# Softplus taken from its table on h itself, 64-bit weights converted with a Prelu, a shift and a join, and a new order of the work

## The chip, the cores and the metric

The kernel runs on one core of one Trainium2 chip. The metric is device time in microseconds (us) of one execution; lower is better. A core has a matrix engine (TensorE, called PE in the profile; PEld is its weight load, which overlaps PE), a vector engine (VectorE, DVE), a scalar engine for activations (ScalarE, ACT), a general engine (GpSimd, POOL) and a queue that issues DMAs (SyncE, SP). Each engine works through its own instructions in the order in which the program lists them; semaphores hold an instruction until what it needs is there.

## The reference

Attention with a forget gate, then two MLPs over its output. Batch 4, 8 heads, 576 positions, head size 64; 2304 tokens of width 512; hidden width 2048. The MLP weights come as 64-bit floating point numbers.

```python
scores = scale * q @ k.T + (cum[:, None] - cum[None, :])   # cum = cumsum(log(clip(f, 1e-4, 1)))
attn = softmax(where(causal, -1e9, scores))
x = attn @ v                                               # to [2304, 512]
h = x @ w_in;  g = maximum(h, 0) + alpha * minimum(h, 0);  x = g @ w_out
h = x @ w_in2; g = maximum(h, 0) + log1p(exp(-abs(h)));    out = g @ w_out2
```

The last `g` is softplus(h).

## The kernel before

The 32 heads are worked in 16 pairs (`pair`, 9 query tiles each). A tile gets its scores from PE, the decay from POOL, the row maximum from DVE (line 643), the exponential `p` from ACT (line 651); PE turns `p` (line 660), and the turned tile is split into a rounded part and a rest (lines 681 and 685), which PE multiplies with `v` (line 725).

The MLPs work on chunks of 384 tokens (6 chunks, three of them from the first half of the batch) and on groups of 4 blocks of 128 hidden units. One slot is one block of one chunk. `hidden` computes `h` in PSUM by 12 matmuls (line 889, the same count in both MLPs), applies the nonlinearity, and splits the result into `g`: ACT casts the rounded part (line 925), DVE subtracts it for the rest (line 928). `product` multiplies `g` with `wout` (line 946): 128x384 per matmul in the first MLP, 9 matmuls of 128x512 a slot in the second. `total` adds the groups (lines 965, 967). The second MLP has 96 slots; in its stage there are 3 PSUM banks for `h` and 6 buffers for `g`. The first three chunks of the first MLP run beside the second half of attention.

In the second MLP the nonlinearity is softplus: DVE sets the sign bit of `h` (line 911, result `ta`, that is -|h|), ACT applies the Softplus table to `ta` (line 915), DVE adds max(h, 0) (line 918).

`weights` turns 64-bit weights into a rounded 32-bit part and a rest. One conversion handles 128x512 numbers: a DMA to `raw` (lines 386, 391); ACT scales the upper words by 2^-112 (`lower`, line 394, result `ca`); DVE shifts (line 397, result `cu`) and joins the sign (line 401); ACT rounds `cu` into the first part (line 413); DVE takes the bits below out of the words (line 405), joins them with the lower word (line 409), takes the power of two (line 416) and multiplies (line 420). There are 64 conversions: 32 for each MLP. Those of the first MLP are also stored to DRAM and read again for the second half of the chunks.

The order is set by a planner (`Plan`). Each step has an engine, a length, the things that it reads and writes, and a rank made from the numbers of `TUNE`. `emit` runs a clock: each free engine takes the step of lowest rank whose inputs are there and for whose results there is a buffer. What comes out is a fixed list for each engine. The planner has no step for a load of activation tables; such a load is put in when the program is built, ahead of an activation whose function is not in the table that is loaded.

```python
        plan.add("act", t_act(512), lower, reads=[rkey], writes=[ua], rank=rank)
        plan.add("dve", t_dve(512, True), shift, reads=[ua], writes=[uu], rank=rank, port=True)
```

Of the kernel before, what the change touches and what calls it, by code (L numbers as in the profile page):

```python
# [7 lines left out]
F32 = mybir.dt.float32  # L8
F32R = mybir.dt.float32r
BF16 = mybir.dt.bfloat16  # L10
U32 = mybir.dt.uint32
# [7 lines left out]


TUNE = {
    "TILE1": 0.42, "TILE2": 0.47, "SLOT2": 7.65, "SLOT3": 13.68, "qr": (-5.98, -0.1), "kr": (0.68, -0.52),
    "vr": (-1.32, 560.85), "cum": (11.69, 8.14), "q": (-1.09, -699.23), "k": (-3.93, -2.73),
    "v": (8.47, 0.66), "decay": (-1.18, 0.77), "scores": (0.88, 3.13), "max": (-8.47, 0.3),
    "pad": (-25.9, 9.39), "exp": (79.74, 1.39), "turn": (-0.12, -0.34), "hi": (1.38, 0.0),
    "lo": (2.49, -2.45), "values0": (16.5, 0.87), "values1": (148.3, 515.38), "sum": (3.42, -0.84),
    "finish": (-1.52, 37.07), "sums": (-1.34, -5.25), "blocks": 6.2, "product": 14.59, "total": 1.13,
    "weights": -0.99, "raw": -0.0, "mlp": -1.66,
}


# [164 lines left out]
def t_act(cols, extra=0, sbuf=True):  # L196
    return (0.094 if sbuf else 0.053) + cols / 1200.0 + 0.093 * extra
# [6 lines left out]
def t_dve(cols, fast=False):  # L204
    return 0.07 + cols / (1920.0 if fast else 960.0)
# [11 lines left out]
def forgetting_attention_two_mlps(  # L217
# [43 lines left out]
            "d": [0, 1, 2, 3], "p": [0, 1, 2, 3], "mx": [0, 1, 2, 3], "sm": [0, 1], "xt0": [0], "xt1": [0], "x32": [0, 1], "r": [0],  # L261
            "rd": [0, 1], "rb": [0], "pt": list(range(8)), "ahead": [0, 1, 2, 3],
            **{"P%d%d%d" % (t, x, n): [0] for t in range(len(UNITS)) for x in range(2) for n in range(2)},
            "raw": [0, 1], "ca": [0, 1], "cu": [0, 1], "win": list(range(5)),
            "wout": [], "h": [], "o": [], "g": [], "ta": [],
        },
        ("p", "d", ("pt", "s"), "win", "wout", "raw"),
# [49 lines left out]
    def buf(key):  # L317
        return tiles[key[0], plan.place[key]]
# [43 lines left out]
    def weights(kind, m, ff, key, rank):  # L362
# [5 lines left out]
        if m == 0 and (kind, ff) in kept:  # L368
# [4 lines left out]

            plan.add("sp", 1.3, again, reads=[saved], writes=[key], rank=rank + DUE["raw"], late=2.92)
            return
        rkey, ua, uu = ("raw", key), ("ca", key), ("cu", key)

        def parts():
            words = buf(rkey).bitcast(U32).rearrange("p (n two) -> p n two", two=2)
            halves = buf(rkey).bitcast(U16).rearrange("p (n four) -> p n four", four=4)  # L380
            return words[:, :, 0], words[:, :, 1].bitcast(F32), halves[:, :, 2]

        def load():
            r = buf(rkey)
# [6 lines left out]
                nc.sync.dma_start(out=r, in_=W[m][1][ff * 128:ff * 128 + 128, :])  # L391

        def lower():
            nc.scalar.mul(out=buf(ua), in_=parts()[1], mul=2.0 ** -112)  # L394

        def shift():
            nc.vector.tensor_scalar(out=buf(uu), in0=buf(ua).bitcast(U32), scalar1=3, scalar2=0x7FFFF000,
                                    op0=ALU.logical_shift_left, op1=ALU.bitwise_and)

        def join():  # L400
            nc.vector.scalar_tensor_tensor(out=buf(uu), in0=parts()[1].bitcast(U32), scalar=0x80000000, in1=buf(uu),
                                           op0=ALU.bitwise_and, op1=ALU.bitwise_or)

        def fraction():
            nc.vector.tensor_scalar(out=buf(ua).bitcast(U32), in0=parts()[1].bitcast(U32), scalar1=511, scalar2=None,
                                    op0=ALU.bitwise_and)

        def tail():
            nc.vector.scalar_tensor_tensor(out=buf(ua), in0=buf(ua).bitcast(U32), scalar=2.0 ** 32, in1=parts()[0],  # L409
                                           op0=ALU.mult, op1=ALU.add)  # L410

        def high():
            nc.scalar.copy(out=buf(key)[0], in_=buf(uu).bitcast(F32))

        def power():
            nc.vector.tensor_scalar(out=buf(uu), in0=buf(uu), scalar1=0xFF800000, scalar2=None,
                                    op0=ALU.bitwise_and)

        def low():
            nc.vector.scalar_tensor_tensor(out=buf(key)[1], in0=buf(ua), scalar=2.0 ** -52, in1=buf(uu).bitcast(F32),  # L420
                                           op0=ALU.mult, op1=ALU.mult)

        plan.add("sp", 0.65, load, reads=[("begun", 1)], writes=[rkey], rank=rank + DUE["raw"], late=1.46)
        plan.add("act", t_act(512), lower, reads=[rkey], writes=[ua], rank=rank)
        plan.add("dve", t_dve(512, True), shift, reads=[ua], writes=[uu], rank=rank, port=True)
        plan.add("dve", t_dve(512), join, reads=[rkey], writes=[uu], rank=rank, port=True)
        plan.add("act", t_act(512), high, reads=[uu], writes=[key], rank=rank)
        plan.add("dve", t_dve(512, True), fraction, reads=[rkey], writes=[ua], rank=rank, port=True)
        plan.add("dve", t_dve(512), tail, reads=[rkey], writes=[ua], rank=rank, port=True)
        plan.add("dve", t_dve(512, True), power, writes=[uu], rank=rank, port=True)  # L430
        plan.add("dve", t_dve(512), low, reads=[ua, uu], writes=[key], rank=rank, port=True)
        if m == 0:
            kept.add((kind, ff))
            if ff < NFF - G:
# [440 lines left out]
    def hidden(it, j):  # L875
# [6 lines left out]
        def hb():  # L882
            return buf(hk)[:, 0:CH]
# [9 lines left out]
        if m == 0:  # L893

            def under():
                nc.scalar.activation(out=buf(ka), in_=hb(), func=AF.Relu, scale=-1.0)  # L896

            def over():
                nc.scalar.activation(out=hb(), in_=hb(), func=AF.Relu)  # L899

            def whole():
                nc.vector.scalar_tensor_tensor(out=hb(), in0=buf(ka), scalar=slope[:, ff:ff + 1], in1=hb(),  # L902
                                               op0=ALU.mult, op1=ALU.add)

            plan.add("act", t_act(CH, sbuf=False), under, reads=[hk], writes=[ka], rank=rank)
            plan.add("act", t_act(CH, sbuf=False), over, reads=[ka], writes=[hk], rank=rank)
            plan.add("dve", t_dve(CH) + 0.06, whole, reads=[ka, ("alpha",)], writes=[hk], rank=rank)
        else:

            def minus():  # L910
                nc.vector.tensor_scalar(out=buf(ka).bitcast(U32), in0=hb().bitcast(U32), scalar1=0x80000000, scalar2=None,  # L911
                                        op0=ALU.bitwise_or)

            def soft():
                nc.scalar.activation(out=buf(ka), in_=buf(ka), func=AF.Softplus)  # L915

            def whole():
                nc.vector.scalar_tensor_tensor(out=hb(), in0=hb(), scalar=0.0, in1=buf(ka), op0=ALU.max, op1=ALU.add)  # L918

            plan.add("dve", t_dve(CH), minus, reads=[hk], writes=[ka], rank=rank)  # L920
            plan.add("act", t_act(CH), soft, writes=[ka], rank=rank)
            plan.add("dve", t_dve(CH), whole, reads=[ka], writes=[hk], rank=rank)

        def hi():
            nc.scalar.copy(out=buf(kg)[0], in_=hb())  # L925
# [79 lines left out]
    with tc.manual_schedule():  # L1005
# [1 line left out]
        left = ctx.enter_context(tc.tile_pool(name="left", bufs=1))  # L1007
        chunk_tiles(left, range(NA))
        slots(left, "raw", range(2), [128, 512], U64)
        slots(left, "ca", range(2), [128, 512])  # L1010
        slots(left, "cu", range(2), [128, 512], U32)
        slots(left, "win", range(5), [128, 512], F32R, 2)
        es_base, es_extra = ExitStack(), ExitStack()
        attention_slots(*open_pools(es_base, "base", "right"), False)
# [197 lines left out]
```

## Time and profile before

| what | us |
|---|---|
| median of 3 runs | 1039.47 |
| lowest and highest run | 1036.82 and 1041.52 |
| span of the profiled execution, first to last instruction | 1035.1 |
| PE busy in the span | 1022.3 |
| DVE busy | 725.1 |
| ACT busy | 518.5 |
| POOL busy | 240.3 |

The profiled execution's own time is not listed apart from the runs; beside its span stands the median, 4.4 us longer, which is what lies around the first and the last instruction. Busy time of PE counts a matmul until its end, and matmuls overlap, so a short wait can be hidden in it. The waits are listed by who waited and who ended the wait.

### The profile page before, as it was taken

The numbers are of one execution on the slowest core, as the hardware profiler recorded it, in microseconds if no ns is written. First come the engines' busy times: TensorE is split into PE (matmuls) and PEld (weight loads), VectorE is DVE, ScalarE is ACT, GpSimd is POOL, SyncE is SP. The second block draws the span as 40 slices with busy tenths as digits, with TensorE's granted clock in tenths as the row PEclk, the third lists the DMA queues.
The fourth block names the chain that finished last, engine by engine and source line by source line (L and its number), as shares of the span: only waits on it lengthen the run. The fifth ranks groups of instructions, "written<-read, shape, count | busy, mean of one in ns | idle before, by whom it ended". The sixth has DMA issues, their size and how long they took to land.

```text
span 1035.1 us, 17156 instructions
## 1 busy us (share of the span) xinstructions
PE 1022.3 (99%) x6023; PEld 946.4 (91%) x6023; DVE 725.1 (70%) x1605; ACT 518.5 (50%) x1264; POOL 240.3 (23%) x399
## 2 busy tenths in 40 slices
PE   8899999999999999999999999999999999999998
PEld 6678899999999899999999999999999998999997
DVE  5898789979999988532335488738765885685543
ACT  6778777776767655344333354434522332332221
POOL 7677766355566520000000000000000000000000
PEclk8999999999999999999999999999999999999999
DMA  7676446646654248020412221202110211010102
GB/s 185 158 225 176 106 124 198 196 147 184 198 167 144 92 159 288 18 71 32 142 40 84 82 61 34 69 1 82 39 45 1 82 41 42 1 41 1 61 31 91
DMA packets 114021, 101.94 MB, mean 98 GB/s; under 512 B 66624, under 2 KB 87248, under 8 KB 113936
## 3 DMA queue, kind: packets, MB, share of 16 engines
q1 hardware_dynamic: 113936, 100.86, 32.3%
q8 instruction: 47, 0.77, 0.3%
q14 instruction: 38, 0.31, 0.1%
HBM read 78.66 MB, written 22.17 MB: 97 GB/s over the span
## 4 chain that ended last, share of the span: by engine, by line
PE 81%; DVE 7%; ACT 4%; issue 3%; POOL 3%; DMA 2%; POOLq 0%; ACTq 0%; DVEq 0%; SPq 0%
PE o L946 36%; PE h L889 35%; PE pt L725 3%; PE pt L621 3%; PE pt L660 2%; POOL d L599 2%; ACT p L651 1%; PE pt L508 1%; DVE d L643 1%; DMA raw<-in_moe_w_in_dram 1%; PE pt L634 1%; DVE p01l L685 1%; DVE ca L409 1%; DVE g L928 1%; DVE acc L967 1%
## 5 line engine op out<-in xcount | busy, mean ns | idle before, releaser
L946 PE MATMUL o<-g,wout 128*128 128x384 f32 x1152 | 213.6, 337 | 0.0
L946 PE MATMUL o<-wout,g 128*128 128x512 f32 x864 | 205.2, 391 | 0.0
L946 PEld LDWEIGHTS o<-g,wout 128*128 128x128 f32 x1152 | 199.4, 188 | 2.3 <-issue 1.9
L946 PEld LDWEIGHTS o<-wout,g 128*128 128x128 f32 x864 | 161.5, 188 | 32.0
L925 ACT CAST g<-h 128x384 fp32r<-128x384 f32 x192 | 92.2, 481 | 141.4 <-PE o L946 126.7
L928 DVE TENSOR_TENSOR g<-h,g 128x384 fp32r<-128x384 f32 x192 | 106.2, 554 | 80.6 <-ACT g L925 79.8
L599 POOL TENSOR_SCALAR d<-cumb,cumc 64x576 f32<-64x576 f32 (+4 forms) x160 | 117.8, 740 | 96.2 <-ACT p L651 90.9
L915 ACT ACTIVATE ta<-ta 128x384 f32<-128x384 f32 x96 | 50.4, 525 | 135.5 <-DVE ta L911 135.2
L902 DVE SCALAR_TENSOR_TENSOR h<-ta,slope,h 128x384 f32<-128x384 f32 x96 | 58.9, 613 | 73.6 <-ACT h L899 73.4
L651 ACT ACTIVATE p<-d,mx 128x128 f32<-128x128 f32 (+2 forms) x144 | 84.4, 588 | 25.8 <-DVE mx L643 24.8
L896 ACT ACTIVATE ta<-h 128x384 f32<-128x384 f32 x96 | 47.3, 492 | 95.2 <-PE h L889 94.6
L911 DVE TENSOR_SCALAR ta<-h 128x384 uint32<-128x384 uint32 x96 | 53.3, 555 | 39.5 <-PE h L889 39.5
L918 DVE SCALAR_TENSOR_TENSOR h<-h,ta 128x384 f32<-128x384 f32 x96 | 54.2, 564 | 38.1 <-ACT ta L915 37.9
L643 DVE CUSTOM_DVE_ANT_0 d<-pt,d 128x128 f32<-128x128 f32 (+2 forms) x144 | 65.3, 477 | 9.7 <-PE pt L626 4.6
L967 DVE TENSOR_TENSOR acc<-o,acc 128x512 f32<-128x512 f32 (+1 forms) x102 | 60.3, 621 | 16.8 <-PE o L946 16.6
L660 PE MATMUL pt<-ident,p 128*128 128x128 f32 (+1 forms) x400 | 65.1, 281 | 4.7 <-ACT p L651 4.3
L660 PEld LDWEIGHTS pt<-ident,p 128*128 128x128 f32 (+1 forms) x400 | 45.7, 140 | 12.3 <-ACT p L651 7.8
L889 PE MATMUL h<-x1h,win 128*128 128x384 f32 x256 | 54.8, 339 | 0.9 <-DVE g L928 0.9
L889 PE MATMUL h<-x2h,win 128*128 128x384 f32 x256 | 55.3, 340 | 0.1
L394 ACT ACTIVATE ca<-raw 128x512 f32<-128x512 f32 x64 | 43.1, 675 | 24.3 <-DMA raw<-in_moe_w_in_dram 11.6
L889 PE MATMUL h<-x0h,win 128*128 128x384 f32 x256 | 54.9, 339 | 0.3 <-DVE g L928 0.3
L889 PE MATMUL h<-x5h,win 128*128 128x384 f32 x256 | 53.5, 335 | 0.0
(157 smaller groups left out, 1909.8 us busy)
## 6 DMA issues: line engine op xcount, KB each, us to landing
raw<-in_moe_w_in_dram SPq DMA_DIRECT2D x32, 512.0 KB, 3.7
raw<-in_moe_w_out_dram SPq DMA_DIRECT2D x32, 512.0 KB, 3.7
cumb<-cum_d SPq DMA_DIRECT2D x30, 288.0 KB, 4.5
out_dram<-acc SPq DMA_DIRECT2D x18, 256.0 KB, 2.1
qr<-in_q_dram SPq DMA_DIRECT2D x32, 128.0 KB, 2.4
vr<-in_v_dram SPq DMA_DIRECT2D x32, 128.0 KB, 2.9
kr<-in_k_dram SPq DMA_DIRECT2D x32, 128.0 KB, 3.3
rb<-rd SPq DMA_DIRECT2D x32, 128.0 KB, 2.9
```

What stands on the lines that cost most here:

```text
L599: nc.gpsimd.tensor_scalar(out=buf(dk)[r, 0:w], in0=buf(cb)[r, hh, 0:w], scalar1=-1.0, scalar2=cumc[r, e, i:i + 1], op0=ALU.mult, op1=ALU.add,)
L643: nc.vector.tensor_tensor_reduce(out=d[:, c0:c1], in0=buf(key)[:, 0:c1 - c0], in1=d[:, c0:c1], scale=-1.0, scalar=least, op0=ALU.add, op1= ...
L651: nc.scalar.activation(out=buf(pk)[:, 0:w], in_=buf(dk)[:, 0:w], func=AF.Exp, bias=buf(mk)[:, x:x + 1], scale=-1.0, accum_out=buf(sm)[:, e ...
L660: nc.tensor.transpose(out=buf(tk[x])[0:rows, (j - j0) * 128:(j - j0) * 128 + 128], in_=buf(pk)[:, j * 128:j * 128 + rows], identity=ident,)
L889: nc.tensor.matmul(out=hb(), lhsT=w_[:, kk * 128:kk * 128 + 128], rhs=x_[:, kk, :], start=(s == 0), stop=(s == len(ops) - 1))
L902: nc.vector.scalar_tensor_tensor(out=hb(), in0=buf(ka), scalar=slope[:, ff:ff + 1], in1=hb(), op0=ALU.mult, op1=ALU.add)
L911: nc.vector.tensor_scalar(out=buf(ka).bitcast(U32), in0=hb().bitcast(U32), scalar1=0x80000000, scalar2=None, op0=ALU.bitwise_or)
L918: nc.vector.scalar_tensor_tensor(out=hb(), in0=hb(), scalar=0.0, in1=buf(ka), op0=ALU.max, op1=ALU.add)
L925: nc.scalar.copy(out=buf(kg)[0], in_=hb())
L928: nc.vector.tensor_sub(buf(kg)[1], hb(), buf(kg)[0].bitcast(F32))
L946: nc.tensor.matmul(out=buf(ok)[:, 0:width], lhsT=a, rhs=b_, start=(j == 0 and s == 0), stop=(j == G - 1 and s == 2))
L967: nc.vector.tensor_add(buf(ok)[:, 0:width] if inner else ac(), buf(ok)[:, 0:width], ac())
```

## The change

Three things change. The softplus is now one ACT instruction on `h` in PSUM; the two DVE instructions and the tile `ta` of the second MLP's slots are not used. The conversion scales the upper words with a Prelu, whose slope for negative numbers, -2^32, turns the sign into one more bit of the exponent; a shift by 3 brings it to its place, the top three bits of the lower word are joined in, and the rest is the difference to the rounded part. The pair of buffers `ca` goes, `cu` has four. And the numbers in `TUNE` are new, so the planner lists the steps in another order. Two rows of that table stand for all.

```diff
--- before.py
+++ after.py
 TUNE = {
-    "TILE1": 0.42, "TILE2": 0.47, "SLOT2": 7.65, "SLOT3": 13.68, "qr": (-5.98, -0.1), "kr": (0.68, -0.52),
...
+    "TILE1": 0.386, "TILE2": 0.486, "SLOT2": 7.049, "SLOT3": 11.393, "qr": (-35.23, -0.39),
...
@@ -261,7 +261,7 @@
             "d": [0, 1, 2, 3], "p": [0, 1, 2, 3], "mx": [0, 1, 2, 3], "sm": [0, 1], "xt0": [0], "xt1": [0], "x32": [0, 1], "r": [0],
             "rd": [0, 1], "rb": [0], "pt": list(range(8)), "ahead": [0, 1, 2, 3],
             **{"P%d%d%d" % (t, x, n): [0] for t in range(len(UNITS)) for x in range(2) for n in range(2)},
-            "raw": [0, 1], "ca": [0, 1], "cu": [0, 1], "win": list(range(5)),
+            "raw": [0, 1], "cu": [0, 1, 2, 3], "win": list(range(5)),
             "wout": [], "h": [], "o": [], "g": [], "ta": [],
         },
         ("p", "d", ("pt", "s"), "win", "wout", "raw"),
@@ -373,12 +373,11 @@
 
             plan.add("sp", 1.3, again, reads=[saved], writes=[key], rank=rank + DUE["raw"], late=2.92)
             return
-        rkey, ua, uu = ("raw", key), ("ca", key), ("cu", key)
+        rkey, uu = ("raw", key), ("cu", key)
 
         def parts():
             words = buf(rkey).bitcast(U32).rearrange("p (n two) -> p n two", two=2)
-            halves = buf(rkey).bitcast(U16).rearrange("p (n four) -> p n four", four=4)
-            return words[:, :, 0], words[:, :, 1].bitcast(F32), halves[:, :, 2]
+            return words[:, :, 0], words[:, :, 1].bitcast(F32)
 
         def load():
             r = buf(rkey)
@@ -391,44 +390,29 @@
                 nc.sync.dma_start(out=r, in_=W[m][1][ff * 128:ff * 128 + 128, :])
 
         def lower():
-            nc.scalar.mul(out=buf(ua), in_=parts()[1], mul=2.0 ** -112)
+            nc.scalar.activation(out=buf(uu), in_=parts()[1], func=AF.Prelu, scale=2.0 ** -112, alpha=-(2.0 ** 32))
 
         def shift():
-            nc.vector.tensor_scalar(out=buf(uu), in0=buf(ua).bitcast(U32), scalar1=3, scalar2=0x7FFFF000,
-                                    op0=ALU.logical_shift_left, op1=ALU.bitwise_and)
-
-        def join():
-            nc.vector.scalar_tensor_tensor(out=buf(uu), in0=parts()[1].bitcast(U32), scalar=0x80000000, in1=buf(uu),
-                                           op0=ALU.bitwise_and, op1=ALU.bitwise_or)
-
-        def fraction():
-            nc.vector.tensor_scalar(out=buf(ua).bitcast(U32), in0=parts()[1].bitcast(U32), scalar1=511, scalar2=None,
-                                    op0=ALU.bitwise_and)
-
-        def tail():
-            nc.vector.scalar_tensor_tensor(out=buf(ua), in0=buf(ua).bitcast(U32), scalar=2.0 ** 32, in1=parts()[0],
-                                           op0=ALU.mult, op1=ALU.add)
+            w = buf(uu).bitcast(U32)
+            nc.vector.tensor_scalar(out=w, in0=w, scalar1=3, scalar2=None, op0=ALU.logical_shift_left)
+
+        def fill():
+            w = buf(uu).bitcast(U32)
+            nc.vector.scalar_tensor_tensor(out=w, in0=parts()[0], scalar=29, in1=w, op0=ALU.logical_shift_right,
+                                           op1=ALU.bitwise_or)
 
         def high():
-            nc.scalar.copy(out=buf(key)[0], in_=buf(uu).bitcast(F32))
-
-        def power():
-            nc.vector.tensor_scalar(out=buf(uu), in0=buf(uu), scalar1=0xFF800000, scalar2=None,
-                                    op0=ALU.bitwise_and)
+            nc.scalar.copy(out=buf(key)[0], in_=buf(uu))
 
         def low():
-            nc.vector.scalar_tensor_tensor(out=buf(key)[1], in0=buf(ua), scalar=2.0 ** -52, in1=buf(uu).bitcast(F32),
-                                           op0=ALU.mult, op1=ALU.mult)
+            nc.vector.tensor_sub(buf(key)[1], buf(uu), buf(key)[0].bitcast(F32))
 
         plan.add("sp", 0.65, load, reads=[("begun", 1)], writes=[rkey], rank=rank + DUE["raw"], late=1.46)
-        plan.add("act", t_act(512), lower, reads=[rkey], writes=[ua], rank=rank)
-        plan.add("dve", t_dve(512, True), shift, reads=[ua], writes=[uu], rank=rank, port=True)
-        plan.add("dve", t_dve(512), join, reads=[rkey], writes=[uu], rank=rank, port=True)
+        plan.add("act", t_act(512) + 0.15, lower, reads=[rkey], writes=[uu], rank=rank)
+        plan.add("dve", t_dve(512, True), shift, writes=[uu], rank=rank, port=True)
+        plan.add("dve", t_dve(512) + 0.1, fill, reads=[rkey], writes=[uu], rank=rank, port=True)
         plan.add("act", t_act(512), high, reads=[uu], writes=[key], rank=rank)
-        plan.add("dve", t_dve(512, True), fraction, reads=[rkey], writes=[ua], rank=rank, port=True)
-        plan.add("dve", t_dve(512), tail, reads=[rkey], writes=[ua], rank=rank, port=True)
-        plan.add("dve", t_dve(512, True), power, writes=[uu], rank=rank, port=True)
-        plan.add("dve", t_dve(512), low, reads=[ua, uu], writes=[key], rank=rank, port=True)
+        plan.add("dve", t_dve(512), low, reads=[uu], writes=[key], rank=rank, port=True)
         if m == 0:
             kept.add((kind, ff))
             if ff < NFF - G:
@@ -907,19 +891,10 @@
             plan.add("dve", t_dve(CH) + 0.06, whole, reads=[ka, ("alpha",)], writes=[hk], rank=rank)
         else:
 
-            def minus():
-                nc.vector.tensor_scalar(out=buf(ka).bitcast(U32), in0=hb().bitcast(U32), scalar1=0x80000000, scalar2=None,
-                                        op0=ALU.bitwise_or)
-
             def soft():
-                nc.scalar.activation(out=buf(ka), in_=buf(ka), func=AF.Softplus)
-
-            def whole():
-                nc.vector.scalar_tensor_tensor(out=hb(), in0=hb(), scalar=0.0, in1=buf(ka), op0=ALU.max, op1=ALU.add)
-
-            plan.add("dve", t_dve(CH), minus, reads=[hk], writes=[ka], rank=rank)
-            plan.add("act", t_act(CH), soft, writes=[ka], rank=rank)
-            plan.add("dve", t_dve(CH), whole, reads=[ka], writes=[hk], rank=rank)
+                nc.scalar.activation(out=hb(), in_=hb(), func=AF.Softplus)
+
+            plan.add("act", t_act(CH, sbuf=False), soft, writes=[hk], rank=rank)
 
         def hi():
             nc.scalar.copy(out=buf(kg)[0], in_=hb())
@@ -1007,8 +982,7 @@
         left = ctx.enter_context(tc.tile_pool(name="left", bufs=1))
         chunk_tiles(left, range(NA))
         slots(left, "raw", range(2), [128, 512], U64)
-        slots(left, "ca", range(2), [128, 512])
-        slots(left, "cu", range(2), [128, 512], U32)
+        slots(left, "cu", range(4), [128, 512])
         slots(left, "win", range(5), [128, 512], F32R, 2)
         es_base, es_extra = ExitStack(), ExitStack()
         attention_slots(*open_pools(es_base, "base", "right"), False)
```

The built program lists 1162 instructions on ACT where there were 1122, and 1223 on DVE where there were 1607; PE (6077), SP (461) and POOL (404) keep their counts. Of ACT's, 42 are table loads; there were 2.

ACT in the second MLP before the change, where weights are being converted (line 394 is the conversion's first step, 413 its rounding, 915 the softplus, 925 the cast of `g`):

```order
L413 CAST wout_0_1978<-cu_0_90 128x512
L925 CAST g_0_1989<-h_0_1998 128x384
L413 CAST wout_0_1970<-cu_0_89 128x512
L394 ACTIVATE ca_0_88<-raw_0_85 128x512
L394 ACTIVATE ca_0_87<-raw_0_86 128x512
L915 ACTIVATE ta_0_4986<-ta_0_4986 128x384
L413 CAST win_0_93<-cu_0_90 128x512
L915 ACTIVATE ta_0_1996<-ta_0_1996 128x384
L925 CAST g_0_1991<-h_0_4991 128x384
L925 CAST g_0_1993<-h_0_1997 128x384
L413 CAST win_0_4987<-cu_0_89 128x512
L394 ACTIVATE ca_0_88<-raw_0_85 128x512
```

The same place in the program now (line 393 is the Prelu, 405 the rounding, 895 the softplus on `h`, 900 the cast of `g`):

```order
L895 ACT_TABLE_LOAD
L895 ACTIVATE h_0_1977<-h_0_1977 128x384
L405 CAST win_0_91<-cu_0_89 128x512
L900 CAST g_0_1964<-h_0_4861 128x384
L393 ACT_TABLE_LOAD
L393 ACTIVATE cu_0_89<-raw_0_86 128x512
L900 CAST g_0_1966<-h_0_1976 128x384
L895 ACT_TABLE_LOAD
L895 ACTIVATE h_0_4861<-h_0_4861 128x384
L405 CAST win_0_93<-cu_0_88 128x512
L393 ACT_TABLE_LOAD
L393 ACTIVATE cu_0_88<-raw_0_85 128x512
```

A load stands now ahead of each Prelu that follows a softplus, and ahead of each softplus that follows a Prelu.

DVE at the same place before (line 405, 409, 416 and 420 belong to the conversion, 911 and 918 to the softplus, 928 is the subtraction for `g`, 967 the sum of the groups):

```order
L416 TENSOR_SCALAR cu_0_90<-cu_0_90 128x512
L409 SCALAR_TENSOR_TENSOR ca_0_88<-ca_0_88,raw_0_85 128x512
L918 SCALAR_TENSOR_TENSOR h_0_1998<-h_0_1998,ta_0_1996 128x384
L420 SCALAR_TENSOR_TENSOR win_1_94<-ca_0_88,cu_0_90 128x512
L928 TENSOR_TENSOR g_1_1992<-h_0_4991,g_0_1991 128x384
L967 TENSOR_TENSOR acc_4985<-o_0_4993,acc_4985 128x512
L401 SCALAR_TENSOR_TENSOR cu_0_89<-raw_0_86,cu_0_89 128x512
L928 TENSOR_TENSOR g_1_1994<-h_0_1997,g_0_1993 128x384
L967 TENSOR_TENSOR acc_4985<-o_0_4994,acc_4985 128x512
L405 TENSOR_SCALAR ca_0_87<-raw_0_86 128x512
L967 TENSOR_TENSOR acc_4985<-o_0_1999,acc_4985 128x512
L911 TENSOR_SCALAR ta_0_1995<-h_0_4991 128x384
```

and now (397 is the shift, 401 the join, 408 the rest of the weights, 903 the subtraction for `g`, 942 the sum):

```order
L903 TENSOR_TENSOR g_1_1965<-h_0_4861,g_0_1964 128x384
L397 TENSOR_SCALAR cu_0_89<-cu_0_89 128x512
L401 SCALAR_TENSOR_TENSOR cu_0_89<-raw_0_86,cu_0_89 128x512
L903 TENSOR_TENSOR g_1_1967<-h_0_1976,g_0_1966 128x384
L408 TENSOR_TENSOR win_1_94<-cu_0_88,win_0_93 128x512
L397 TENSOR_SCALAR cu_0_88<-cu_0_88 128x512
L942 TENSOR_TENSOR acc_4853<-o_0_1979,acc_4853 128x512
L408 TENSOR_TENSOR win_1_4858<-cu_0_89,win_0_4857 128x512
L942 TENSOR_TENSOR acc_4853<-o_0_1978,acc_4853 128x512
L903 TENSOR_TENSOR g_1_1969<-h_0_1977,g_0_1968 128x384
```

Nothing of the softplus is left on DVE, and a conversion has three instructions; a shift and a join stand between two subtractions for `g`.

## Rows read from the trace of the kernel before

**Rows 1.** The page's first part: busy time, share of the span, instructions of each engine.
```profile
PE 1022.3 (99%) x6023; PEld 946.4 (91%) x6023; DVE 725.1 (70%) x1605; ACT 518.5 (50%) x1264; POOL 240.3 (23%) x399
```

**Rows 2.** Busy time by stretch: PE, PEld, DVE, ACT, POOL; PE clock, DMA share, GB/s.
```profile
0.00:50.00 50.00, 44.57 (x299) 33.87 (x299) 37.03 (x114) 33.92 (x102) 35.11 (x71) 0.90 0.65 172
50.00:130.00 80.00, 78.80 (x632) 66.68 (x630) 67.37 (x203) 63.31 (x199) 62.12 (x104) 1.00 0.62 168
130.00:400.00 270.00, 267.75 (x1742) 250.99 (x1742) 245.49 (x578) 191.55 (x496) 143.03 (x225) 1.00 0.54 165
400.00:1015.00 615.00, 614.90 (x3287) 581.80 (x3286) 368.99 (x702) 228.26 (x466) 0.00 (x0) 1.00 0.17 54
1015.00:1035.10 20.10, 16.24 (x72) 13.09 (x70) 6.26 (x10) 1.49 (x3) 0.00 (x0) 1.00 0.23 86
```

**Rows 3.** Waits of PE and its weight loads: total us, times, longest us.
```profile
PEld pt L660 <- ACT p L651: 7.8, 16, 2.9
...
PEld h L889 <- DVE g L928: 2.8, 6, 0.8
```

**Rows 4.** Timeline 38 to 46 us, ACT then PE: start us, length us, instruction [idle before <-releaser].
```profile
42.94 0.66 ACT L394 ACTIVATE ca<-raw 128x512 f32<-128x512 f32 x1 [3.37 <-DMA raw<-in_moe_w_in_dram]
43.51 0.76 ACT L651 ACTIVATE p<-d,mx 128x576 f32<-128x576 f32 x1
...
44.41 0.77 PE L660 MATMUL pt<-ident,p 128*128 128x128 f32 x5 [2.73 <-ACT p L651]
```

**Rows 5.** Timeline of one period of the second MLP, ACT, DVE, PE.
```profile
844.30 0.48 ACT L925 CAST g<-h 128x384 fp32r<-128x384 f32 x1 [0.82 <-PE o L946]
846.34 0.48 ACT L925 CAST g<-h 128x384 fp32r<-128x384 f32 x1 [1.56 <-PE o L946]
...
852.60 0.48 ACT L925 CAST g<-h 128x384 fp32r<-128x384 f32 x1 [0.77 <-PE o L946]
...
845.16 0.55 DVE L928 TENSOR_TENSOR g<-h,g 128x384 fp32r<-128x384 f32 x1
...
846.85 0.56 DVE L928 TENSOR_TENSOR g<-h,g 128x384 fp32r<-128x384 f32 x1
...
846.08 0.87 PE L889 MATMUL h<-x1h,win 128*128 128x384 f32 x4
...
848.19 0.85 PE L889 MATMUL h<-x2h,win 128*128 128x384 f32 x4
```

**Rows 6.** Groups by line and shape: busy us, mean ns of one | idle before it.
```profile
L405 DVE TENSOR_SCALAR ca<-raw 128x512 uint32<-128x512 uint32 x64 | 30.8, 481 | 0.1
L409 DVE SCALAR_TENSOR_TENSOR ca<-ca,raw 128x512 f32<-128x512 uint32 x64 | 46.9, 734 | 0.6
L416 DVE TENSOR_SCALAR cu<-cu 128x512 uint32<-128x512 uint32 x64 | 28.1, 439 | 4.2 <-ACT win L413 3.7
L401 DVE SCALAR_TENSOR_TENSOR cu<-raw,cu 128x512 uint32<-128x512 uint32 x64 | 44.7, 698 | 0.5
L911 DVE TENSOR_SCALAR ta<-h 128x384 uint32<-128x384 uint32 x96 | 53.3, 555 | 39.5 <-PE h L889 39.5
L918 DVE SCALAR_TENSOR_TENSOR h<-h,ta 128x384 f32<-128x384 f32 x96 | 54.2, 564 | 38.1 <-ACT ta L915 37.9
L394 ACT ACTIVATE ca<-raw 128x512 f32<-128x512 f32 x64 | 43.1, 675 | 24.3 <-DMA raw<-in_moe_w_in_dram 11.6
L413 ACT CAST win<-cu 128x512 fp32r<-128x512 f32 x32 | 19.8, 620 | 8.7 <-PE h L889 6.0 <-DVE cu L401 2.5
L899 ACT ACTIVATE h<-h 128x384 f32<-128x384 f32 x96 | 46.8, 488 | 0.0
```

**Rows 7.** Timeline of ACT around the table load ahead of the first softplus.
```profile
618.51 0.48 ACT L975 CAST x3h<-o 128x384 fp32r<-128x384 f32 x1 [1.29 <-DVE o L967]
619.01 1.28 ACT L915 ACT_TABLE_LOAD   x1
620.98 0.53 ACT L915 ACTIVATE ta<-ta 128x384 f32<-128x384 f32 x1 [0.68 <-DVE ta L911]
```

## What the change is expected to do

> **What bounds the kernel now.** I read the busy shares first, then the same by stretch, then who waits for whom, then single queues. The page's first part [rows 1] shows TensorE (PE) busy for 1022.3 of 1035.1 us, VectorE (DVE) for 725.1 and ScalarE (ACT) for 518.5. The stretches [rows 2] say where PE is not busy: 5.43 us up to 50 us, 1.20 up to 130, 2.25 up to 400, only 0.10 between 400 and 1015, and 3.86 in the last 20 us. The change takes no matmul away, so nothing that it saves on DVE or ACT after 400 us can shorten the run; there is only something to lose there. What can be won lies before 400 us, where attention runs. PE's matmuls overlap, so a wait can hide inside busy time; the waits for data that PE and its weight loads show [rows 3] are a second measure: the largest are 7.8 us for `p` (the exponentials of line 651) and 2.8 us for `g` (line 928). The one long stall of 2.73 us near 44 us has its cause on ACT's queue [rows 4]: a weight conversion (line 394) stood first in the queue and waited 3.37 us for its DMA, and the softmax that PE wanted stood behind it.
>
> From 650 us on the second MLP repeats a period of two slots, 8.30 us long (from the cast of `g` at 844.30 to the one at 852.60, [rows 5]). The order in a period is two `h` products, then two products that use `g`. ACT casts `g` the moment PE frees its buffer, DVE subtracts, and the `h` bank is then free for PE. That chain has little slack: the subtraction that starts at 845.16 ends at 845.71 and PE enters at 846.08, 0.37 us later; the next one ends at 847.41 and PE enters at 848.19, 0.78 us later. So PE loses nothing now, but a cast that is late by more than 0.4 to 0.8 us stops PE.
>
> **The change, part by part.**
>
> *Weight conversion on DVE.* 64 conversions lose lines 405, 409 and 416: 481 + 734 + 439 = 1654 ns each, 105.9 us of DVE [rows 6]. The shift, the join (priced as line 401, 698 ns) and the last subtraction stay at about what lines 397, 401 and 420 take. 32 of the 64 run before 400 us: 53 us less DVE there out of 349.9 busy (37.03 + 67.37 + 245.49). This is the part that can gain. Bounds: nothing, if the waits are not DVE's doing; or all of the 7.8 + 2.8 = 10.6 us. I take 4 us, nearer the lower half: six of the 32 fall before 130 us, where most of PE's idle time is, and the longest stall was a DMA's. The other half of the saving falls under busy PE and is worth 0; the cover is PE's own work, which has no gap there.
>
> *Softplus.* 96 times lines 911 and 918 go: 555 + 564 ns, 107.4 us of DVE, all after 615 us, worth 0. The softplus in PSUM I price as the Relu in PSUM, 488 ns.
>
> *Prelu for the multiplication.* Nothing before shows it. Nearest row: line 394, 675 ns for the same strided read. Bounds: that, and about 1.05 us if it went through ACT as two halves (675 plus half of it).
>
> *The table loads.* This is what the diff does not show. The order of ACT has 42 table loads where there were 2: Softplus and Prelu are in different tables, so wherever a conversion stands between two softplus a load stands ahead of each. All 40 new ones lie after 600 us. One load is 1283 ns [rows 7], so 51.3 us of ACT are added. By the average that fits: ACT is busy 228.3 of 615 us. In a window it does not. A dense period, as the second listing of the order shows it, holds 4 loads (5.13), 2 conversions (1.35), 2 casts of weights (1.24), 2 softplus (0.98) and 2 casts of `g` (0.96): 9.66 us in a period of 8.30. Walked through, with the first cast at 0: cast to 0.48, load to 1.76, conversion to 2.44; the second cast is due at 2.04, so 0.40 late, which the slack takes; cast to 2.92, load to 4.20, softplus to 4.69, weight cast to 5.31, load to 6.59, conversion to 7.27, load to 8.55, softplus to 9.04, weight cast to 9.66; the next cast was due at 8.30 and is 1.36 late. Less a slack of 0.4 to 0.8, PE stands for 0.6 to 1.0 us. I carried the same walk through all the places, where a stall of PE also moves what is due next: about 0.7 us where the second MLP begins, 3.4 near slots 22 to 25 of the 96 and 1.5 near 31 and 32, 1.7 near 46 to 49 and 1.2 near 55 to 57, 8.5 in all. On DVE the shift and the join of a conversion now stand ahead of the subtraction of `g` (0.44 + 0.70 us, a conversion's end being late); I add 1.5 us for that. Sum: 10 us lost.
>
> What is uncertain is the time between a load's end and the next instruction. Ahead of the load there is none: the cast before it ends at 618.99 and the load starts at 619.01. After it 0.68 us pass until 620.98, but a wait for DVE ended them [rows 7], so 0 and 0.68 are the bounds. The walk with 0.68 gives 27 us lost instead of 8.5. I take 0, since DVE's result came 0.02 us ahead of the softplus and explains all of the wait. The Trainium skill (ScalarE: Activation LUTs, What ACT_TABLE_LOAD costs) says that every switch costs 1283 ns for the load and about 1380 ns for a drain, 2.66 us together, by which the walk would give 50 us lost. The trace agrees on the load's 1283 ns; a drain is not seen ahead of the load, and after it there was room for 0.68 us at most.
>
> *The order chosen anew.* PE has the same 5939 matmuls and changes between kinds of work 312 times before and after; 816 instead of 840 matmuls of the first MLP stand ahead of the last of attention. SP and POOL keep 461 and 404 instructions. I count 0, with 3 us either way: [rows 4] shows what one badly placed conversion costs, 2.73 us, and it can go or come.
>
> Sum against the profiled execution: span 1035.1, minus 4, plus 10, gives 1041.1. Its own full time is not listed beside the runs; their median, 1039.47, lies 4.4 us over the span, which I leave as it is. Forecast 1045.5 us; with the bounds of the small terms, 1041 to 1051.
>
> **The rivals.**
>
> *No change.* The loads fall into the idle time of ACT because DVE, 107 us lighter, returns `g` sooner, and every margin is 0.8 rather than 0.4. Then 4 to 6 us are lost and 4 won: 1039 to 1041, down to 1035 if the order is good too. For it: slack of 0.78 in half the cases. Against it: the walk is late by 1.36.
>
> *Faster.* One mechanism: DVE's queue is what makes `p` late before 130 us (DVE is busy 67.4 of 80 us from 50 to 130). With it gone most of the 10.6 us and the 2.73 us stall go, 13 us, against at most 6 for the loads: 1032. It decides where PE waits less than 3 us in all before 400 us. Against: most single waits are short, and only six conversions lie there.
>
> *Late ACT.* Something stands after a load, or Prelu takes 1.05 us (the walk then gives 14 us). Between that and 0.68 us after each load (27 us by the walk): 1051 to 1064.
>
> *A long switch.* The engine stops around a load for as long again as the load takes, so that a switch costs two loads, 2.57 us. A dense period then holds 5.1 us more, PE stands at every place where a load is, and the walk gives 47 us lost: 1039.5 - 4 + 47 + 1.5 = 1084. Against it: no idle time ahead of the load in [rows 7], and at most 0.68 us behind it. The Trainium skill's section named above is the rule that speaks for it.
>
> *The change doesn't do what it says*: if the scheduler had grouped the conversions, there would be few loads; the order shows 42, so this has no chance of its own.
>
> **How the numbers follow.** Half a per cent, about what a measurement of this kernel can tell from no change, is 5.2 us: 1034.3 to 1044.7. Chances: forecast 0.47, of which 0.29 above 1044.7; no change 0.20; faster 0.12; late ACT 0.14; the long switch 0.07. Slower: 0.29 + 0.14 + 0.07 = 0.50; same: 0.18 + 0.20 = 0.38; faster 0.12. The range leaves out the faster case and the long switch, 0.19, and the far end of late ACT: 1035 to 1062.
>
> **What would show it.** Right: 42 loads of 1.28 us on ACT; PE idle after 600 us in a few lumps of 0.3 to 2 us, 8 to 12 us in all, ended by the subtraction of `g`; none between 420 and 600 us; DVE busy some 210 us less; PE's idle time before 400 us at 4 to 6 us instead of 8.9. Wrong: idle time ahead of the softplus after each load (late ACT or the long switch); PE without a gap after 600 us (no change); less than 3 us of PE idle before 400 us (faster); a gap of over 2 us that a DMA ended before 400 us (the new order).

## The result, and the profile after

The changed kernel takes 1043.12 us, median of 16 runs; the kernel before takes 1037.49 in as many. The ratio is 1.0053, with a 95% interval from 1.0042 to 1.0065: slower by 5.6 us, just over half a per cent, with an interval that begins just under it. The forecast was 1045.5 against a median of 1039.47 for before, 6.0 us slower.

The 4.4 us between span and time that the forecast carried along are not what lies around the first and the last instruction: wherever time and span of one execution are both on record, they differ by 2.2 us in the kernel before and by 1.7 us in the changed kernel. The profiled execution before thus took about 1037.3 us, and the median of three runs came from slower ones.

Busy time by stretch in the changed kernel, in the columns of [rows 2]:

```profile
0.00:50.00 50.00, 46.94 (x339) 36.78 (x340) 39.42 (x119) 39.27 (x119) 38.27 (x80) 0.97 0.76 193
50.00:130.00 80.00, 79.09 (x631) 66.55 (x630) 62.43 (x197) 60.30 (x191) 57.52 (x102) 1.00 0.64 168
130.00:400.00 270.00, 268.93 (x1741) 253.60 (x1741) 208.91 (x497) 190.56 (x492) 124.02 (x218) 1.00 0.59 183
400.00:600.00 200.00, 200.00 (x1156) 200.00 (x1155) 85.23 (x155) 80.57 (x179) 0.00 (x0) 1.00 0.20 64
600.00:1015.00 415.00, 407.21 (x2068) 369.49 (x2067) 138.20 (x243) 188.70 (x319) 0.00 (x0) 1.00 0.11 34
```

PE is without work for 3.06 + 0.91 + 1.07 = 5.04 us before 400 us, where [rows 2] gave 8.88, and for 7.79 us from 600 to 1015 us, where there had been 0.10. DVE is busy 541.9 us in the span instead of 725.1. That is 183.2 us less, not the 210 expected, though the five lines that went had 213.3 us by their own rows [rows 6]: DVE's instructions overlap where they follow at once (below, the join of 812.75 ends at 813.44 and the next starts at 813.36), and busy time counts the overlap once. So attention won something and the second MLP lost more.

The waits of PE and its weight loads, as in [rows 3]:

```profile
PEld h L873 <- DVE g L903: 13.2, 16, 2.0
PE h L873 <- DVE g L903: 7.6, 13, 1.7
...
PEld pt L644 <- ACT p L635: 3.8, 12, 0.7
```

The wait for `p` fell from 7.8 to 3.8 us. The wait for `g`, 2.8 before, is 13.2: the `h` product waits for the subtraction (line 903) that frees its PSUM bank.

The groups of ACT that are new (busy us, mean ns of one, idle before):

```profile
L895 ACT ACTIVATE h<-h 128x384 f32<-128x384 f32 x96 | 45.4, 475 | 114.7 <-PE h L873 114.5
L393 ACT ACTIVATE cu<-raw 128x512 f32<-128x512 f32 x64 | 42.9, 672 | 7.9 <-DVE wout L408 4.2 <-DVE win L408 1.4 <-DMA raw<-in_moe_w_out_dram 1.2
L895 ACT ACT_TABLE_LOAD x21 | 26.9, 1283 | 0.4
L393 ACT ACT_TABLE_LOAD x20 | 25.7, 1283 | 0.4
```

The Prelu costs what the scaling did, 672 against 675 ns [rows 6], the softplus in PSUM 475 ns. The loads are there, 52.6 us of them on these two lines, 1283 ns each.

One dense period on ACT:

```profile
807.62 1.28 ACT L895 ACT_TABLE_LOAD   x1
808.91 0.47 ACT L895 ACTIVATE h<-h 128x384 f32<-128x384 f32 x1
809.29 0.61 ACT L405 CAST win<-cu 128x512 fp32r<-128x512 f32 x1
809.80 0.48 ACT L900 CAST g<-h 128x384 fp32r<-128x384 f32 x1
810.30 1.28 ACT L393 ACT_TABLE_LOAD   x1
811.60 0.66 ACT L393 ACTIVATE cu<-raw 128x512 f32<-128x512 f32 x1
812.16 0.47 ACT L900 CAST g<-h 128x384 fp32r<-128x384 f32 x1
812.65 1.28 ACT L895 ACT_TABLE_LOAD   x1
813.94 0.47 ACT L895 ACTIVATE h<-h 128x384 f32<-128x384 f32 x1
...
819.14 0.48 ACT L900 CAST g<-h 128x384 fp32r<-128x384 f32 x1
```

ACT has no gap from one first cast of `g` to the next, 809.80 to 819.14: 9.34 us in place of the period of 8.30 [rows 5]. DVE and PE beside it:

```profile
812.29 0.43 DVE L397 TENSOR_SCALAR cu<-cu 128x512 uint32<-128x512 uint32 x1 [1.20 <-ACT cu L393]
812.75 0.69 DVE L401 SCALAR_TENSOR_TENSOR cu<-raw,cu 128x512 uint32<-128x512 uint32 x1
813.36 0.55 DVE L903 TENSOR_TENSOR g<-h,g 128x384 fp32r<-128x384 f32 x1
```

```profile
811.15 0.96 PE L873 MATMUL h<-x5h,win 128*128 128x384 f32 x4 [0.36 <-DVE g L903]
...
813.97 0.97 PE L873 MATMUL h<-x5h,win 128*128 128x384 f32 x4 [0.46 <-DVE g L903]
...
821.08 0.96 PE L873 MATMUL h<-x0h,win 128*128 128x384 f32 x4 [0.63 <-DVE g L903]
```

The cast at 812.16 ends at 812.63, but its subtraction starts at 813.36, behind the shift and the join of the conversion that ended just before. It ends at 813.91 and PE enters at 813.97. Each of the three `h` products waits 0.4 to 0.6 us on the profile's account. From 9.66 us in the walk to 9.34 here is again overlap: the rounding of 809.29 would end at 809.90, and the cast starts at 809.80.

### The profile page after: what moved, and what is told of

It reads as the page before. It is cut to its first block, busy times and chain, and to the rows that moved or that the text cites. A ratio compares the mean times of both kernels' runs of the same rounds, so it can differ in the third digit from the quotient of the medians.

```text
span 1040.1 us, 16757 instructions
## 1 busy us (share of the span) xinstructions
PE 1023.4 (98%) x6023; PEld 944.1 (91%) x6023; DVE 541.9 (52%) x1221; ACT 561.8 (54%) x1304; POOL 219.8 (21%) x399
## 4 chain that ended last, share of the span: by engine, by line
PE 82%; ACT 9%; DVE 3%; issue 2%; DMA 2%; POOL 1%; SPq 0%; ACTq 0%; DVEq 0%; POOLq 0%
PE h L873 35%; PE o L921 33%; PE pt L709 5%; PE pt L644 3%; PE pt L605 3%; ACT L393 2%; PE pt L618 1%; ACT cu L393 1%; PE pt L492 1%; ACT L895 1%; ACT p L635 1%; DMA qr<-in_q_dram 1%; DVE d L627 1%; ACT win L405 1%; ACT wout L405 1%
## 5 line engine op out<-in xcount | busy, mean ns | idle before, releaser
L583 POOL TENSOR_SCALAR d<-cumb,cumc 128x128 f32<-128x128 f32 (+4 forms) x160 | 101.2, 636 | 105.6 <-ACT p L635 92.5
L895 ACT ACTIVATE h<-h 128x384 f32<-128x384 f32 x96 | 45.4, 475 | 114.7 <-PE h L873 114.5
L942 DVE TENSOR_TENSOR acc<-o,acc 128x512 f32<-128x512 f32 (+1 forms) x102 | 62.8, 625 | 75.2 <-PE o L921 75.0
L873 PE MATMUL h<-x3h,win 128*128 128x384 f32 x256 | 52.7, 335 | 0.0
L873 PE MATMUL h<-x4h,win 128*128 128x384 f32 x256 | 52.5, 335 | 0.0
L873 PEld LDWEIGHTS h<-x0h,win 128*128 128x128 f32 x256 | 44.3, 188 | 6.3 <-DVE g L903 5.7
```

Source lines behind the costliest of these rows:

```text
L583: nc.gpsimd.tensor_scalar(out=buf(dk)[r, 0:w], in0=buf(cb)[r, hh, 0:w], scalar1=-1.0, scalar2=cumc[r, e, i:i + 1], op0=ALU.mult, op1=ALU.add,)
L873: nc.tensor.matmul(out=hb(), lhsT=w_[:, kk * 128:kk * 128 + 128], rhs=x_[:, kk, :], start=(s == 0), stop=(s == len(ops) - 1))
L895: nc.scalar.activation(out=hb(), in_=hb(), func=AF.Softplus)
L942: nc.vector.tensor_add(buf(ok)[:, 0:width] if inner else ac(), buf(ok)[:, 0:width], ac())
```

## The experiments

Times are medians; ratios are against runs of the kernel before on the same chip, with the 95% interval.

| run | us | ratio | PE without work 0 to 400 / 600 to 1015 us |
|---|---|---|---|
| before | 1037.49 | 1 | 8.88 / 0.10 |
| changed kernel | 1043.12 | 1.0053 (1.0042 to 1.0065) | 5.04 / 7.79 |
| e1_copy | 1031.78 | 0.9941 (0.9920 to 0.9962) | 7.06 / 0.27 |
| e2_sign_dve | 1032.04 | 0.9943 (0.9922 to 0.9965) | 5.58 / 0.00 |
| e3_old_order | 1049.26 | 1.0108 (1.0088 to 1.0129) | 8.26 / 7.83 |
| e4_new_order | 1043.60 | 1.0061 (1.0038 to 1.0084) | 13.82 / 0.00 |
| e5_softplus_alone | 1037.70 | 0.9995 (0.9979 to 1.0010) | 9.95 / 0.00 |
| e6_sign_old_order | 1037.61 | 0.9996 (0.9981 to 1.0010) | 10.01 / 0.00 |
| e7_loads_planned | 1037.03 | 0.9987 (0.9974 to 0.9999) | 9.99 / 0.00 |
| e8_half_the_loads | 1038.97 | 1.0009 (0.9998 to 1.0020) | 5.25 / 5.87 |
| e9_loads_planned_later | 1030.96 | 0.9942 (0.9924 to 0.9960) | 5.62 / 0.00 |

The last column is read from one execution of each. Up to 400 us the changed kernel, e1, e8 and e9 run the same instructions, and PE is without work there for 5.04, 7.06, 5.25 and 5.62 us, so a difference of 2 us in that column says nothing of the order. Part of it is PE's clock: up to 50 us it is granted at 1.00 in e1, with PE busy for 45.29 us, and at 0.97 in the changed kernel, with PE busy for 46.94 us. At the lower clock the same work fills time in which PE would else wait.

**Without the loads, e1_copy.**

```diff
         def lower():
+            if m == 1:
+                nc.scalar.mul(out=buf(uu), in_=parts()[1], mul=2.0 ** -112)
+                return
             nc.scalar.activation(out=buf(uu), in_=parts()[1], func=AF.Prelu, ...
```

> The changed kernel with one edit: in the 32 conversions of the second MLP's weights the Prelu is a plain scaling copy, so the sign of these weights is left out. No table load stands between softplus and conversion any more (2 loads in all instead of 42), and every other instruction keeps its place. Theory (the loads fill ACT in the dense windows, the cast of g comes late, PE stands): PE's 7.8 us without work between 600 and 1015 us fall below 0.5, the time falls by 9 to 11 us to 1032 to 1034 us. Rival (the order chosen anew is what opens the gaps, the shift and join ahead of the subtraction of g): 4 us of idle time or more stay there, 1038 to 1042 us.

It measured 1031.78 us, just below what was expected. The lists of instructions are those of the changed kernel but for the 40 loads and the copy in the Prelu's place, so the loads cost 1.0053 - 0.9941 = 1.1% of the time, 11.6 us; the spans say 1040.1 - 1028.9 = 11.2. The gaps after 600 us go but for 0.27 us. The rival, that the order itself opens them, falls.

**The whole computation without the loads, e2_sign_dve.** As e1, and the sign by one DVE instruction:

```diff
+            if m == 1:
+                nc.vector.tensor_scalar(out=w, in0=w, scalar1=3, scalar2=0x7FFFFFFF, op0=ALU.logical_shift_left,
+                                        op1=ALU.bitwise_and)
+                return
...
+        def sign():
+            w = buf(uu).bitcast(U32)
+            nc.vector.scalar_tensor_tensor(out=w, in0=parts()[1].bitcast(U32), scalar=0x80000000, in1=w,
+                                           op0=ALU.bitwise_and, op1=ALU.bitwise_or)
```

> As the run before, but with the whole computation: the sign comes back by one more DVE instruction (32 of about 0.70 us, 22 us of DVE in the second MLP), the first MLP's weights keep the Prelu. Theory (DVE has room there): 1032 to 1035 us, faster than both kernels. Rival (DVE's queue is what makes the subtraction of g late): PE idle after 600 us of 2 us or more, 1036 to 1041 us.

It measured 1032.04 us, faster than both kernels. Busy by stretch:

```profile
0.00:400.00 400.00, 394.42 (x2707) 356.43 (x2708) 313.79 (x816) 290.10 (x801) 218.69 (x399) 1.00 0.62 180
400.00:600.00 200.00, 200.00 (x1155) 200.00 (x1155) 87.48 (x159) 81.02 (x180) 0.00 (x0) 1.00 0.20 64
600.00:1015.00 415.00, 415.00 (x2125) 380.73 (x2123) 158.14 (x275) 139.88 (x283) 0.00 (x0) 1.00 0.12 37
```

DVE is 20 us busier after 600 us than in the changed kernel (158.14 against 138.20) and PE has no gap there. In e1 the shift and the join stand ahead of the same subtractions as in the changed kernel, and PE loses next to nothing. What stood ahead of the subtraction on DVE thus mattered only because ACT was late.

**Lighter load or new order.** Two runs exchange the table of numbers (`TUNE`), e3_old_order and e4_new_order:

> The changed instructions with the table of numbers of before, so the planner makes another order of them; Softplus and Prelu still share ACT. If the gain before 400 us comes from DVE's lighter load: PE idle there 4 to 6 us, as in the changed kernel. If it comes from the order: 8 to 10 us. By both the loads cost 8 to 12 us after 600 us: 1041 to 1045 us by the first, 1045 to 1049 by the second.

> The instructions of before with the new table of numbers, no loads beyond two. If the gain before 400 us comes from DVE's lighter load: PE idle there 8 us or more, 1037 to 1040 us, like before. If it comes from the order: 4 to 6 us of PE idle there, 1032 to 1035 us.

e3 measured 1049.26 us, just above the range of the second of the two cases, with that case's PE idle before 400 us, 8.26 us. e4 measured 1043.60 us, which neither case had: with the instructions of before, the new numbers make attention worse.

```profile
0.00:400.00 400.00, 386.18 (x2603) 344.16 (x2604) 341.56 (x877) 278.26 (x777) 231.71 (x399) 0.98 0.55 159
```

That is 13.82 us without work, in an execution that took 1048.07 us, the slowest of e4's seven. By the medians the new numbers alone cost 6 us. The other half is e6_sign_old_order, the lighter load with old numbers and without the loads of tables (the table of numbers of before put into e2):

> The version with the sign on DVE, no new loads, and the table of numbers of before. What is left against before is DVE's lighter load without the new numbers. If the lighter load makes the gain in attention by itself: 1031 to 1034 us. If it takes the new numbers too: 1035 to 1040 us; the run with old numbers and loads, 1049 us, less 11 for the loads, points to 1038.

It measured 1037.61 us, ratio 0.9996, with 10.01 us of PE idle before 400 us. Neither half gains by itself; together (e2) they gain 6. The lighter load here is all that the new conversion brings: three instructions of DVE less, and four buffers `cu` in place of two `ca` and two `cu`. Which of the two counts, and which of the numbers, was not tried, and each order is one sample of what the planner can make. e3 and e6 price the loads a second time, in another order: 1.0108 - 0.9996 = 1.1%, 11.6 us again.

**The softplus alone, e5_softplus_alone** (the last hunk of the diff in the kernel before):

> The kernel before with the new softplus alone: one ACT instruction on h in place of DVE, ACT, DVE, 107 us of DVE less in the second MLP; conversions and table of numbers as before, two loads. Theory (PE has no gap there that DVE could close): the same as before within 2 us, 1036 to 1040 us. Rival (the lighter DVE gives margin back or the clock differs): 1030 to 1034 us.

It measured 1037.70 us, ratio 0.9995. About 100 us less DVE work after 600 us (181.89 busy against 281.43) are worth nothing there.

**Half of the loads, e8_half_the_loads** (`if m == 1 and kind == 1` in the edit of e1).

> The changed kernel; the 16 conversions of w_out of the second MLP use the scaling copy (the sign of these weights is left out), those of w_in keep the Prelu, so 18 of the 40 loads stay. If each window pays for itself, as the walk has it, what is left is the loss near slots 22 to 25 and 46 to 49 and part of that where the second MLP begins, 5 to 7 us of 11: 1036 to 1039 us. If a loss moves on to the next window: 1040 us or more.

It measured 1038.97 us. Against e1 (0.9941) 0.68% are left, 7.1 us, of 11.6 with all loads: just above the 5 to 7 us expected. PE's gaps stay where the conversions of w_in are and go where those of w_out were.

**A planner that knows of the loads, e7_loads_planned and e9_loads_planned_later.**

```diff
-        plan.add("act", t_act(512) + 0.15, lower, ...
+        plan.add("act", t_act(512) + 0.15 + (2.6 if m == 1 else 0.0), lower, ...
```

> The changed kernel, with the planner told that a conversion in the second MLP costs ACT 2.6 us more, the two loads. 38 loads stay. If the loss comes from loads that the planner doesn't know, it now leaves room for them: PE idle from 600 to 1015 us 1 to 3 us instead of 7.8, 1033 to 1037 us. If ACT is simply too full in these windows for any order: 1040 to 1044 us.

It measured 1037.03 us. From 600 to 1015 us PE has no gap at all, with 38 of the 40 loads in, so the second case, ACT too full there for any order, falls. But it came out at the top of the range, since PE waited 3.7 us for `g` near 370 and 392 us, in a part where no load runs, and a slow piece of 3.4 us followed each wait (last section): the longer step also changed the plan for the first conversions of the second MLP's weights, which run beside attention's end. e9 leaves these four alone: `if m == 1 and (kind == 1 or ff >= G)`.

> As the run in which the planner knows of the loads, but the first group's four conversions of w_in keep their old length, since they run before any softplus and have no load. PE's list is then that of the changed kernel through all of attention. Theory (the 3.7 us for g near 370 and 392 us of that run were an accident of its changed order, and the loads themselves can be hidden whole): PE idle 5 to 6 us before 400 us, below 2 us from 600 to 1015 us, 1031 to 1035 us, with 38 loads in. Rival (loads hidden in the second MLP are paid for elsewhere): 1036 us or more.

It measured 1030.96 us, ratio 0.9942. The table loads of this run, and its stretches:

```profile
L895 ACT ACT_TABLE_LOAD x20 | 25.7, 1283 | 0.4
L393 ACT ACT_TABLE_LOAD x19 | 24.4, 1283 | 0.3
```

```profile
0.00:400.00 400.00, 394.38 (x2707) 356.58 (x2708) 310.95 (x812) 289.72 (x801) 219.67 (x399) 1.00 0.62 181
...
600.00:1015.00 415.00, 415.00 (x2126) 380.98 (x2125) 140.53 (x254) 188.42 (x323) 0.00 (x0) 1.00 0.11 36
```

ACT is as busy after 600 us as in the changed kernel (188.42 and 188.70), and PE loses nothing. The same window as above, in this run:

```profile
808.32 0.48 ACT L900 CAST g<-h 128x384 fp32r<-128x384 f32 x1 [0.41 <-PE o L921]
808.70 0.62 ACT L405 CAST win<-cu 128x512 fp32r<-128x512 f32 x1
810.43 0.48 ACT L900 CAST g<-h 128x384 fp32r<-128x384 f32 x1 [1.11 <-PE o L921]
810.93 1.28 ACT L393 ACT_TABLE_LOAD   x1
```

No load stands between the two casts of `g`, and each cast waits for PE, not PE for it. The loss of the changed kernel is thus not the price of 40 loads but of 40 loads that the planner did not know.

## Why the prediction was right

**The loads.** The step that carried the forecast held: loads of 1283 ns at the places that the order shows, too dense in a few windows, each cast of `g` late, PE standing for the subtraction. The walk gave 9.66 us for a dense period and a first cast 1.36 us late; the trace shows 9.34 between the first casts. PE stood at the slots named: near 22 to 25 (705 to 720 us), 31 and 32 (745 to 752), 46 to 49 (811 to 821), 55 to 57 (848 to 858), and where the second MLP begins. Summed, the loss was put at 10 us and measured 11.6. The traces give it by place. The changed kernel and e1 have the same list on DVE, so the start of one and the same subtraction for `g` (line 903, in e1 line 906) can be compared behind each place:

| behind | start, changed kernel | start, e1 | later by | lost there | the walk |
|---|---|---|---|---|---|
| attention and the first MLP | 609.47 | 609.82 | -0.35 | | |
| the beginning of the second MLP | 671.23 | 668.73 | 2.50 | 2.85 | 0.7 |
| slots 22 to 25 | 733.22 | 726.87 | 6.35 | 3.85 | 3.4 |
| slots 31 and 32 | 769.87 | 762.14 | 7.73 | 1.38 | 1.5 |
| slots 46 to 49 | 838.54 | 828.59 | 9.95 | 2.22 | 1.7 |
| slots 55 to 57 | 873.02 | 861.82 | 11.20 | 1.25 | 1.2 |

Four of the five places come within 0.5 us of the walk. They lose more time than PE's gaps show: from 811 to 821 us the three waits of PE are 1.45 us, those of its weight loads 2.61, and the loss is 2.22: with matmuls that overlap, part of a wait is counted as busy time. So the sign "8 to 12 us of idle time" was just missed, 7.79, with 11.55 us lost. How much of the loss is the 1.5 us added for DVE is not separated by any run.

The term of this sum that was mis-sized is the beginning of the second MLP: the walk gave 0.7 us there and 2.85 were lost. PE waited longest before the matmul at 617.87:

```profile
614.21 1.28 ACT L393 ACT_TABLE_LOAD   x1
615.50 0.66 ACT L393 ACTIVATE cu<-raw 128x512 f32<-128x512 f32 x1
616.07 0.84 ACT L900 CAST g<-h 128x384 fp32r<-128x384 f32 x2
```

```profile
617.87 0.97 PE L873 MATMUL h<-x0h,win 128*128 128x384 f32 x4 [1.66 <-DVE g L903]
```

The cast of `g` came behind a load and a conversion there, and on DVE its subtraction came behind that conversion's shift and join.

**After a load.** The open question was 0 to 0.68 us. It is 0: in the rows above 808.91 follows a load that ends at 808.90, and 811.60 one that ends at 811.58. The rivals of late ACT and of the long switch fall with that. The rule of the Trainium skill (ScalarE: Activation LUTs, What ACT_TABLE_LOAD costs) that a drain of about 1380 ns comes with each switch does not hold in this kernel: behind 38 of its 42 loads the next instruction starts 11 to 12 ns after the load's end. Prelu at 672 ns closes the other half of late ACT, whose bound of 1.05 us should have been 1.01 by its own terms (675 ns and half of it).

**Attention.** The gain was put at 4 us and measured 6.1 (e1 against before). PE's idle time fell by 3.84 us, as forecast, and that agreement is in part luck: in e1, with the same instructions, it fell by 1.82. What the sum lacked is PE's clock. Before, the granted clock up to 50 us is 0.90 [rows 2], 0.97 now, a difference of 3.5 us of work at full speed. Two pieces of the trace before and two of the trace after, in the same columns:

```profile
10.00:20.00 10.00, 8.96 (x58) 5.76 (x56) 5.33 (x22) 6.21 (x22) 7.46 (x15) 0.74 0.88 241
40.00:50.00 10.00, 7.26 (x48) 4.68 (x46) 8.24 (x25) 5.32 (x15) 5.73 (x8) 0.83 0.76 209
```

```profile
10.00:20.00 10.00, 9.38 (x71) 6.27 (x70) 6.53 (x26) 7.25 (x26) 8.43 (x19) 0.90 0.92 245
40.00:50.00 10.00, 9.88 (x83) 8.06 (x82) 9.92 (x29) 9.82 (x30) 9.44 (x14) 1.00 0.73 166
```

The long stall of [rows 4] is gone, and with it the slow piece that followed; that is half of the difference, and the other half lies from 10 to 20 us. Clock and idle time have to be added, since either moves from one execution to the next. Idle time up to 400 us and what the clock took up to 50 us are together 13.9 us before, 11.5 in e5, whose instructions in attention are those of before, and 6.5 to 7.1 us in the changed kernel, e1, e8 and e9. The gain is thus 4 to 7 us, and which part of it is clock can't be told from one execution. The account by spans: -3.8 idle, -3.5 clock, +11.5 loads gives +4.2; measured +5.0 by spans, so about one us stays without a name. The two terms were too small by 2 us each, in opposite directions, which is why the difference of 6.0 us came out closer to the measured 5.6 than either. That the time itself came 2.4 us under the forecast is mostly the median of three that it started from, 2.0 us above that of 16.

**Where the gain comes from** was half wrong. The prediction put it to DVE's lighter load and counted 0 for the order, with 3 us either way. The runs show that neither is right alone: lighter load with the old numbers 0.9996, new numbers with the old load 1.0061, both without the loads 0.9943.

**The softplus** on `h` was counted at 0, and e5 shows 0.9995. **No change** and **faster** would have needed loads that are hidden; e9 shows that they can be, with another order, and then the result, 1031, is near the 1032 of the faster rival. Its mechanism is not what brought it: that rival wanted less than 3 us of PE idle before 400 us, and e9 has 5.62. Its 13 us also counted the stall near 44 us twice, which is part of the 7.8 us in [rows 3].

## What to carry to other kernels

Before a function of the activation engine is exchanged for another, look whether its table is the one that its neighbours in the queue use; where two functions alternate, put the loads into the planner's costs or choose an instruction that needs no load beside its neighbours, as the scaling copy of e1 and e2. Average load says little: ACT was busy under half of the time after 600 us and still made PE wait, since 9.3 us of work stood in a period of 8.3. And a saving and an order belong together: here the lighter conversion gained nothing in the old order, and the new numbers lost 6 us without it, so each has to be tried with the other.

## What the runs showed of the hardware

A load of a table needed no time beside its 1283 ns: about 0.02 us ahead of it and 0.01 behind.

A stall of PE can cost more than its own length, by the clock. In the kernel before PE waits 2.73 us until 44.41 [rows 4], and then runs from 46.0 to 49.4 us at half the clock, the lower of its two levels (1.2 GHz of 2.4):

```profile
44.40:46.00 1.60, 1.59 (x9) 0.90 (x11) 1.44 (x5) 0.90 (x3) 1.46 (x3) 0.99 0.56 129
46.00:49.40 3.40, 3.40 (x19) 1.90 (x15) 3.33 (x9) 2.94 (x10) 3.11 (x4) 0.50 0.57 184
49.40:52.00 2.60, 2.60 (x27) 2.30 (x24) 1.46 (x5) 1.81 (x6) 2.08 (x5) 1.00 0.74 168
```

In e7_loads_planned it happened twice more, at and after the waits for `g` of 1.63 us (until 369.70) and 2.08 us (until 392.31):

```profile
369.00:373.00 4.00, 3.30 (x10) 3.30 (x11) 2.39 (x5) 1.86 (x5) 2.78 (x2) 0.58 0.15 54
373.00:393.00 20.00, 17.92 (x103) 17.60 (x103) 11.24 (x21) 9.53 (x20) 0.04 (x1) 1.00 0.88 294
393.00:397.00 4.00, 4.00 (x16) 4.00 (x15) 0.63 (x2) 0.87 (x2) 0.00 (x0) 0.57 1.09 345
```

It need not happen. In e5_softplus_alone PE waits nearly as long at the same place, and runs on at the full clock:

```profile
43.57 0.77 PE L660 MATMUL pt<-ident,p 128*128 128x128 f32 x5 [2.42 <-ACT p L651]
```

```profile
46.00:50.00 4.00, 4.00 (x36) 3.15 (x35) 3.93 (x12) 4.00 (x13) 4.00 (x5) 1.00 0.55 152
```

The waits of the changed kernel's second MLP, 1.66 us before 617.87 and at most 1.17 us after it, left the clock at 1.00 from 600 to 1015 us:

```profile
719.85 0.96 PE L873 MATMUL h<-x0h,win 128*128 128x384 f32 x4 [1.17 <-DVE g L903]
```

What decides whether the clock falls is open.
